# Attention and MoE on one planned instruction stream: the first batch weighted pair by pair, its pooled V summed in two halves, other staging rooms for incoming weights, and a planner that holds an engine for what is urgent

## The chip, the cores and the metric

The kernel runs on one core of a Trainium2 chip. The metric is the device time of one execution in microseconds (us), lower is better.

## What is computed

The input is q, k and v of 8 batches, 8 heads, 576 tokens and 64 channels in float32, and the weights of an MoE layer of width 512 to 2048 and back. The reference, cut to what matters:

```python
q_d, k_d, v_d = (t.reshape(B, H, 144, 4, D).mean(axis=3) for t in (q, k, v))
out_up = np.repeat(softmax(q_d @ k_d.T / 8) @ v_d, 4, axis=2)        # pooled attention
mask = np.abs(pos[:, None] - pos[None, :]) < 4
out_local = softmax(np.where(mask, q @ k.T / 8, -1e9)) @ v           # seven neighbours
x = (out_up + out_local).transpose(0, 2, 1, 3).reshape(4608, 512)
h = x @ w_in                                                         # 512 -> 2048
P = a[0] + a[1] * h + a[2] * h * h + a[3] * h**3
Q = 1.0 + abs(b[0]) * abs(h) + abs(b[1]) * h * h
out = (P / (Q + 1e-6)) @ w_out                                       # 2048 -> 512
```

The weights arrive as 64-bit floats and are turned into float32 on the chip.

## The kernel before

**A planner writes the order.** Every piece of work is a task with an engine, an estimated duration, the rooms of SBUF and PSUM that it reads and writes, and for some a due time (`add(engine, dur, fn, reads, writes, due)`). `Plan.run` walks back from the due times to a latest start for each task, and then plays the tasks through: whichever engine is free soonest takes, of its tasks whose inputs are ready by the estimates, the one with the earliest latest start. `LAG` and `OWN` are the times that the planner allows between a task and one that needs it; for SP (the DMA queue) that is the time from the end of the issue to the landing. What comes out is a fixed list for each engine, and on the chip each engine takes its list in order: an instruction that has to wait holds up all behind it.

**The MoE half** goes through ten blocks of tokens: 512 tokens of each batch, and the 64 left over of each of four batches together. A block has 16 steps (8 for the small ones). Step n makes 128 rows of h in `h_part` (TensorE, into bank 2 or 3), turns them into g = P/Q in `middle` (ScalarE reads h four times at L705, then VectorE from L720 on), and adds g times its rows of `w_out` to four output banks in `o_part` (L757). Weights and x are split in a high and a low part (`wh` and `wl`, `xs`), and a product is three matmuls. Block 0 is different: its h is a plain float32 matmul (L680) from `xf`, which holds x before the split, and `wb`, the unsplit float32 weight, so it needs neither split. Its four matmuls of a step take the four pairs of heads one after the other.

**The attention half** works on pairs of heads; a batch has four (0 to 3). For a pair: scores (L399, L409), softmax (`nm` on VectorE, exponentials `el` at L456 and `ep` at L482 on ScalarE), normalising on VectorE, turning by TensorE and copying back on ScalarE (`turned`: `ept` L543, `et` L553 and L554), then `weighted`: pooled V by the pooled attention (L579), V windows by the local one (L568), `up` (L625), and the sum of both into `xf` (L611, `put_x`). For batches 1 to 7 this is strewn into the block before. Batch 0 comes first and alone, and until its x is there TensorE has only small work; `warm` fills its gaps with matmuls that nobody reads (L889), by the gaps that the planner foresees.

**Pooled V of batch 0** (`vf`) comes by one load from SP and three adding DMAs from GpSimd (L811), each of which waits for the landing of the one before.

**The weights**: 32 chunks of 512 KB, 16 of `w_in` and 16 of `w_out`, in the order in which the steps need them. `weights` loads a chunk into a staging room (a "spot", L310), ScalarE scales it (L320), VectorE makes the float32 word in two steps (L323, L326) and, for `w_out`, ScalarE and VectorE split it (L340, L343; for `w_in` that comes later, before block 1). The staging rooms are eleven: five (`st`) lie in the rooms `m` and `g` that `middle` uses from step 0 on and serve once, four (`sl`) lie in the rooms of the last weights, two (`sx`) in the room of x of batch 1. After the first nine chunks the rest take turns in the four `sl`, and the last seven in the two `sx`.

Of the kernel before, what the change touches and what calls it, by code (L numbers as in the profile page):

```python
# [76 lines left out]
class Plan:  # L77
# [3 lines left out]
    LAG = {"PE": 0.25, "DVE": 0.14, "ACT": 0.18, "POOL": 0.2, "SP": 2.0}  # L81
# [34 lines left out]

    def run(self):
# [20 lines left out]
        while len(done) < len(self.tasks):  # L138
# [29 lines left out]
def attention_moe(  # L168
# [136 lines left out]
    def weights(w, f, spot, due=None):  # L305
# [62 lines left out]
    def load_pooled(c):

        s, b, i = c.slot, c.b, c.i  # L370
        for dst, src, cost in ((s.pq, qkp, 0.5), (c.vp, vp, 0.4)):
# [184 lines left out]
    def vp_of(c):  # L556
        return vf.ap[:, c.i] if c.b == 0 else c.vp.ap

    def weighted(cs, bk, due):
# [3 lines left out]
        def window(c, x, w, o):  # L563
            g, k = w % 2, w // 2
            nq = min(WQ, S - w * WQ)
            for j in range(2):
                m = c.pos(j) * D
                nc.tensor.matmul(  # L568
                    x.ap[j * D : (j + 1) * D, o : o + nq],
                    lhsT=c.slot.vw.ap[m : m + D, w, :],  # L570
                    rhs=c.slot.et.ap[m : m + D, k, g * D : g * D + nq],
                    start=True, stop=True, skip_group_check=True,
                )

        def part_b():
            for c, x in zip(cs, avb):
                for kc in range(2):
                    for j in range(2):
                        nc.tensor.matmul(  # L579
                            x.ap[j * D : (j + 1) * D, 256 : 256 + SD],  # L580
# [401 lines left out]
```

## Time and profile before

| | |
|---|---|
| median of 3 runs (lowest to highest) | 986.43 us (985.28 to 986.58) |
| the profiled execution | 986.62 us |
| its span, from first to last instruction | 984.9 us |
| TensorE busy (matmuls) | 961.5 us, 98% of the span |
| VectorE, ScalarE busy | 838.9 us (85%), 810.8 us (82%) |
| mean granted TensorE clock | 0.994 |

The profiled execution has 1.7 us outside its span. Times in the views are microseconds from the span's start. PE is TensorE, DVE VectorE, ACT ScalarE, POOL GpSimd, SPq the DMA queue of SP. Busy spans of neighbouring instructions overlap by some 0.1 us, so what an instruction costs in a full stretch is read from start to start.

### The profile page before, as it was taken

To read this page: it belongs to the slowest core of one execution; us is meant where nothing else is said; L and a number is where in the kernel's file an instruction comes from. 1 tells how busy PE (TensorE), PEld (TensorE's weight loads), DVE (VectorE), ACT (ScalarE), POOL (GpSimd) and SP (SyncE) were. 2 spreads that over 40 slices of the span, in tenths; PEclk is the share of its full clock that TensorE was granted. 3 is DMA by queue.
4 is the path that set the end of the run, shared out by engine and by line. 5 is a ranking of instruction groups with operands and counts; after the bars stand their busy time and mean duration, and the time that the engine had idled before them with its cause. 6 is when DMAs were issued, how large, how long until landed. Compare 5 with 4: busy or idle time off the path is not lost.

```text
span 984.9 us, 19800 instructions
## 1 busy us (share of the span) xinstructions
PE 961.5 (98%) x7379; PEld 759.3 (77%) x7379; DVE 838.9 (85%) x1472; ACT 810.8 (82%) x2078; POOL 149.2 (15%) x177
## 2 busy tenths in 40 slices
PE   7799999999999999999999999999999999999997
PEld 5556656788888888988888887888878888898886
DVE  6699999988878978887978898888888888888886
ACT  6789987897989798679797978798887979767775
POOL 1400213122222222001212030302121220000000
PEclk9989999999999999999999999999999999999999
DMA  9964544333443234003334142524233420100001
GB/s 317 297 206 142 143 135 90 89 69 71 74 118 72 68 75 105 1 22 86 64 84 120 57 81 64 107 74 67 84 60 108 74 52 1 44 1 22 1 1 43
DMA packets 46371, 83.43 MB, mean 85 GB/s; under 512 B 6564, under 2 KB 29092, under 8 KB 46276
## 3 DMA queue, kind: packets, MB, share of 16 engines
q1 hardware_dynamic: 25828, 62.70, 19.2%
q0 software_dynamic: 20448, 19.48, 14.3%
q8 instruction: 58, 0.95, 0.4%
q14 instruction: 37, 0.30, 0.1%
HBM read 72.72 MB, written 9.44 MB: 83 GB/s over the span
## 4 chain that ended last, share of the span: by engine, by line
PE 87%; DMA 5%; DVE 3%; ACT 3%; issue 0%; ACTq 0%; SPq 0%
PE psum L757 39%; PE psum L692 36%; PE psum L680 3%; DMA sl<-in_w_out_dram 3%; PE psum L568 2%; PE psum L530 2%; PE psum L579 1%; PE psum L537 1%; PE psum L409 1%; PE psum L426 1%; DMA vw<-in_vw_dram 1%; ACT m L705 1%; DMA sx<-in_w_out_dram 1%; PE psum L399 1%; DVE wl L343 1%; ACT el L456 1%
## 5 line engine op out<-in xcount | busy, mean ns | idle before, releaser
L757 PE MATMUL psum<-wh,g 128*128 128x512 f32 x1152 | 369.3, 402 | 1.2 <-DVE g L738 1.1
L692 PE MATMUL psum<-xs,wh 128*128 128x512 f32 (+1 forms) x1152 | 265.0, 370 | 0.0
L705 ACT ACTIVATE m<-psum,cf 128x512 f32<-128x512 f32 x288 | 218.7, 766 | 40.2 <-PE psum L692 37.5
L757 PEld LDWEIGHTS psum<-wh,g 128*128 128x128 f32 x1152 | 208.8, 188 | 49.2 <-issue 4.8
L692 PEld LDWEIGHTS psum<-xs,wh 128*128 128x128 f32 x1152 | 199.3, 189 | 35.9
L757 PE MATMUL psum<-wl,g 128*128 128x512 f32 x576 | 224.7, 391 | 0.0
L705 ACT ACTIVATE gb<-psum,cf 128x512 f32<-128x512 f32 x144 | 116.4, 808 | 53.4 <-PE psum L757 53.4
L376 POOL DMA_DIRECT2D pq<-in_qkp_dram x84 | 74.7, 924 | 476.0 <-DMA pq<-in_qkp_dram 449.4
L692 PE MATMUL psum<-xs,wl 128*128 128x512 f32 (+1 forms) x576 | 141.5, 367 | 0.0
L729 DVE TENSOR_TENSOR g<-m,m 128x512 fp32r<-128x512 f32 x144 | 99.2, 689 | 42.4 <-ACT m L705 40.0
L720 DVE SCALAR_TENSOR_TENSOR m<-m,cf,m 128x512 f32<-128x512 f32 x144 | 107.6, 747 | 31.5 <-ACT m L705 31.3
L757 PEld LDWEIGHTS psum<-wl,g 128*128 128x128 f32 x576 | 108.1, 188 | 23.6
L456 ACT ACTIVATE el<-psum,nm 128x64 f32<-128x64 f32 x320 | 97.8, 355 | 33.7 <-DVE nm L448 33.4
L726 DVE TENSOR_TENSOR m<-m,gb 128x512 f32<-128x512 f32 x144 | 99.3, 689 | 21.6 <-ACT gb L705 17.0
L692 PEld LDWEIGHTS psum<-xs,wl 128*128 128x128 f32 x576 | 101.3, 189 | 18.9 <-issue 1.2
L705 ACT ACTIVATE gb<-m,cf 128x512 f32<-128x512 f32 x144 | 108.0, 750 | 0.0
L732 DVE SCALAR_TENSOR_TENSOR m<-m,g 128x512 f32<-128x512 f32 x144 | 99.3, 689 | 2.9
L737 DVE TENSOR_TENSOR m<-m,m 128x512 f32<-128x512 f32 x144 | 99.3, 689 | 2.9
L725 DVE TENSOR_TENSOR m<-m,m 128x512 f32<-128x512 f32 x144 | 98.6, 685 | 0.4 <-ACT m L705 0.4
L738 DVE TENSOR_TENSOR g<-m,m 128x512 fp32r<-128x512 f32 x144 | 98.0, 680 | 0.8
L705 ACT ACTIVATE m<-gb 128x512 f32<-128x512 f32 x144 | 94.5, 656 | 2.5
L376 POOL DMA_DIRECT2D vp<-in_vp_dram x84 | 71.6, 916 | 151.7 <-DMA vp<-in_vp_dram 142.8
(66 smaller groups left out, 989.3 us busy)
## 6 DMA issues: line engine op xcount, KB each, us to landing
qk<-in_qk_dram SPq DMA_DIRECT2D x32, 590.0 KB, 5.0
pq<-in_qkp_dram POOLq DMA_DIRECT2D x84, 144.0 KB, 3.3
vw<-in_vw_dram SPq DMA_DIRECT2D x32, 320.0 KB, 3.5
out_dram<-xf SPq DMA_DIRECT2D x32, 256.0 KB, 2.3
vp<-in_vp_dram POOLq DMA_DIRECT2D x84, 72.0 KB, 3.2
sl<-in_w_in_dram SPq DMA_DIRECT2D x10, 512.0 KB, 8.1
sl<-in_w_out_dram SPq DMA_DIRECT2D x10, 512.0 KB, 10.5
pq<-in_qkp_dram SPq DMA_DIRECT2D x28, 144.0 KB, 2.2
```

The lines of the kernel that those rows point to most:

```text
L376: lambda d=dst, x=src, r=r: nc.gpsimd.dma_start(out=d.ap, in_=x[b, r, :, i], accum_op=ALU.add),
L456: nc.scalar.activation(out=s.el.ap[:, k, c.pos(j), :], in_=view[:, j, k, :], func=AF.Exp, bias=nm[:, 5 * j + k : 5 * j + k + 1], scale=sca ...
L692: nc.tensor.matmul(ph.ap[:, f * t : (f + 1) * t], lhsT=(high, low)[j][0][fc].ap[:, c, :], rhs=blk.x[i].ap[:, c, :], start=(part_ == 0 and ...
L705: add("ACT", cost, lambda: nc.scalar.activation(out=out_.ap, in_=in_, func=func, **kw), (room_in, cf, *more), (out_,))
L720: lambda: v.scalar_tensor_tensor(out=tb.ap, in0=tq.ap, scalar=b1, in1=tb.ap, op0=ALU.mult, op1=ALU.add),
L725: add("DVE", 0.61, lambda: v.tensor_tensor(out=ta.ap, in0=ta.ap, in1=tq.ap, op=ALU.mult), (ta, tq), (ta,))
L726: add("DVE", 0.61, lambda: v.tensor_tensor(out=ta.ap, in0=ta.ap, in1=u.ap, op=ALU.add), (ta, u), (ta,))
L729: add("DVE", 0.61, lambda: v.tensor_tensor(out=gh.ap, in0=ta.ap, in1=tq.ap, op=ALU.mult), (ta, tq), (gh,))
L732: lambda: v.scalar_tensor_tensor(out=tb.ap, in0=tb.ap, scalar=CONE, in1=gh.ap.bitcast(F32), op0=ALU.add, op1=ALU.mult),
L737: add("DVE", 0.61, lambda: v.tensor_tensor(out=tb.ap, in0=ta.ap, in1=tb.ap, op=ALU.subtract), (ta, tb), (tb,))
L738: add("DVE", 0.61, lambda: v.tensor_tensor(out=gl.ap, in0=tb.ap, in1=tq.ap, op=ALU.mult), (tb, tq), (gl,))
L757: nc.tensor.matmul(ob[sub].ap, lhsT=g[i].ap[:, f0 : f0 + P], rhs=flat((high, low)[j][1][fc].ap), start=(fc == 0 and m == 0), stop=(fc == N ...
```

## The change

Six things change; line numbers of the changed kernel are some 18 to 40 higher, so L320 is L338 there, L611 is L623, L340 is L358 and L705 is L743.

1. The planner's allowances for SP: 3.0 instead of 2.0 from issue to landing, and 4.5 for a load that starts before 60 (2.5 after); longer issue times for the big loads; 7.0 and 4.0 for the adding DMAs; slightly longer matmuls.
2. `HOLD`: when a task with a latest start at least 15 earlier than the one at hand becomes ready before that one would be done, the engine takes something shorter or is left free for it.
3. `weighted` of batch 0 goes pair by pair (`weighted_pooled`, then `weighted_local` at once), with the banks of `FIRST`.
4. `vf` becomes two tiles; SP loads one quarter of V into each, GpSimd adds one more into each, and `pooled_sums` adds the two halves up by twice as many matmuls (for batch 0 alone).
5. The staging rooms are five `sx` (in the room of the high part of x) and the four `sl`, all nine in turn for all chunks; the last seven chunks take the `sx`. None lies in `m` or `g` now.
6. `SPLIT_EARLY` 8 instead of 6.

```diff
-    LAG = {"PE": 0.25, "DVE": 0.14, "ACT": 0.18, "POOL": 0.2, "SP": 2.0}
+    LAG = {"PE": 0.25, "DVE": 0.14, "ACT": 0.18, "POOL": 0.2, "SP": 3.0}
...
+        if p.engine == "SP" and p.start is not None:
+            return 4.5 if p.start < 60.0 else 2.5
...
+            soon = [
+                (r, w.late) for r, _, w in waiting[e]
+                if r < at + t.dur - HOLD[0] and w.late < t.late - HOLD[1]
+            ]
+            if soon and at < HOLD[2]:
+                r = min(soon)[0]
+                fit = [o for o in open_[e] if at + o[2].dur <= r + HOLD[0]]
+                heapq.heappush(open_[e], (t.late, t.n, t))
+                if not fit:
+                    free[e] = r
+                    continue
+                o = min(fit)
...
-    vf = put("vf", [KC, NPAIR, 2, 2, D], F32, low[0][half].at)
+    vf = [put(f"vf{i}", [KC, NPAIR, 2, 2, D], F32, low[i][half].at) for i in range(2)]
...
-    spots = [put(f"st{i}", [P, 2 * DM], I32, r.at) for i, r in enumerate((mt[0], mt[2], mt[4], gt[0], gt[2]))]
+    spots = [put(f"sx{i}", [P, 2 * DM], I32, at) for i, at in enumerate((
+        xs[0][0].at, xs[0][0].at + 4096, xs[1][0].at, xs[1][0].at + 4096, xs[2][0].at))]
...
-    spots += [put(f"sx{i}", [P, 2 * DM], I32, xs[1][0].at + i * 4096) for i in range(2)]
...
-        add("SP", 1.4, load, (), (spot,), due=due)
+        add("SP", 1.65, load, (), (spot,), due=due)
...
-                    (dst,), (dst,), lag=2.8,
+                    (dst,), (dst,), lag=4.0,
...
+    def pooled_sums(c, x):
+        vs = vp_of(c)
+        for kc in range(2):
+            for n, v in enumerate(vs):
+                for j in range(2):
+                    nc.tensor.matmul(
+                        x.ap[j * D : (j + 1) * D, 256 : 256 + SD],
+                        lhsT=v[:, j, kc, :],
+                        rhs=c.slot.ept.ap[:, kc, :, c.pos(j), :],
+                        start=(kc == 0 and n == 0), stop=(kc == 1 and n == len(vs) - 1), skip_group_check=True,
+                    )
...
+    def weighted_pooled(c, y):
+
+        add("PE", 1.1, lambda: pooled_sums(c, y), (c.slot.ept, *vf), (y,))
+        keep_up(c, y)
+
+    def weighted_local(c, x, y, due):
+        add(
+            "PE", 0.7,
+            lambda: [window(c, x if w < 8 else y, w, w % 8 * WQ) for w in range(NW)],
+            (c.slot.vw, c.slot.et), (x, y),
+        )
+        put_x(c, x, 0, 0, NA, 0.55, due)
+        put_x(c, y, 0, NA, FULL, 0.12, due)
+        put_x(c, y, FULL - NA, FULL, S, 0.13, due)
...
-    spot_of = [spots[i % 9] for i in range(9)] + [spots[5 + i % 4] for i in range(len(order) - 9)]
+    spot_of = [spots[i % 9] for i in range(len(order))]
...
-        spot_of[i] = spots[9 + n % 2]
+        spot_of[i] = spots[n % 5]
...
-    add("SP", 0.8, lambda: nc.sync.dma_start(out=vf.ap, in_=vp[0, 0]), (), (vf,), due=-18)
-    for r in range(1, POOL):
+    for r, x in enumerate(vf):
+        add("SP", 0.8, lambda r=r, x=x: nc.sync.dma_start(out=x.ap, in_=vp[0, r]), (), (x,), due=-18)
         add(
             "POOL", 1.0,
-            lambda r=r: nc.gpsimd.dma_start(out=vf.ap, in_=vp[0, r], accum_op=ALU.add),
-            (vf,), (vf,), lag=4.0,
+            lambda r=r, x=x: nc.gpsimd.dma_start(out=x.ap, in_=vp[0, 2 + r], accum_op=ALU.add),
+            (x,), (x,), lag=7.0,
         )
...
-            turned(c, [bk[n] for n in ((6, 4, 5), (6, 4, 5), (2, 3, 0), (6, 1, 2))[2 * q + i]])
-        weighted(cs, [bk[n] for n in ((4, 5, 4, 5), (1, 2, 0, 3))[q]], due0 - 10.0 * (1 - q))
+            (tp, t0, t1), (x, y) = FIRST[2 * q + i]
+            turned(c, [bk[tp], bk[t0], bk[t1]])
+            weighted_pooled(c, bk[y])
+            weighted_local(c, bk[x], bk[y], due0 - 10.0 * (1 - q))
...
+HOLD = (0.1, 15.0, 2000.0)
+FIRST = (((6, 4, 5), (6, 4)), ((6, 4, 5), (6, 4)), ((2, 3, 0), (2, 3)), ((6, 1, 5), (6, 1)))
```

The first place is ScalarE in the middle of batch 0, behind the last exponentials `el3` (names with their numbers: `el3` is of pair 3, `sl0` and `sx4` are staging rooms). Before:

```order
L456 ACTIVATE el3_219,sm3_190<-psum,nm3_186 128x64 x5
L553 COPY et0_197<-psum 128x512
L320 ACTIVATE sl0_229<-sl0_229 128x512
L554 COPY et0_197<-psum 128x128
L482 ACTIVATE ep3_222,sm3_190<-psum,nm3_186 128x144 x3
L543 COPY ept1_205<-psum 72x288
L482 ACTIVATE ep2_215,sm2_189<-psum,nm2_185 128x144 x3
```

And in the changed kernel, where the scaling of a loaded chunk (L338) has moved behind the exponentials of all pairs:

```order
L474 ACTIVATE el3_219,sm3_190<-psum,nm3_186 128x64 x5
L561 COPY ept0_198<-psum 72x288
L500 ACTIVATE ep2_215,sm2_189<-psum,nm2_185 128x144 x3
L500 ACTIVATE ep3_222,sm3_190<-psum,nm3_186 128x144 x3
L571 COPY et0_197<-psum 128x512
L605 ACTIVATE up0_191<-psum 128x144
L572 COPY et0_197<-psum 128x128
L561 COPY ept2_214<-psum 72x288 x2
L338 ACTIVATE sx4_229<-sx4_229 128x512
```

The second place is VectorE where x of the last pairs is written. Before, the word of a chunk loaded into `sl1` for the second time (L323, L326) stood ahead of the six writes of pairs 2 and 3:

```order
L323 TENSOR_SCALAR wb1_3_127<-sl1_230 128x512
L326 SCALAR_TENSOR_TENSOR wb1_3_127<-sl1_230,wb1_3_127 128x512
L611 TENSOR_TENSOR xf0_1_155<-psum,up0_191 128x48
L611 TENSOR_TENSOR xf2_1_163<-psum,up0_191 128x64
L611 TENSOR_TENSOR xf0_1_155<-psum,up1_192 128x48
L611 TENSOR_TENSOR xf2_1_163<-psum,up1_192 128x64
L611 TENSOR_TENSOR xf0_1_155<-psum,up0_191 128x464
L611 TENSOR_TENSOR xf0_1_155<-psum,up1_192 128x464
```

Now pairs 2 and 1 are written before any chunk that is in its staging room's second turn, and the first such chunk (`sx1`) stands ahead of pair 3 only:

```order
L361 TENSOR_TENSOR wl1_0_120<-wb1_0_121,wh1_0_72 128x512
L623 TENSOR_TENSOR xf0_1_155<-psum,up0_191 128x464
L623 TENSOR_TENSOR xf0_1_155<-psum,up0_191 128x48
L623 TENSOR_TENSOR xf2_1_163<-psum,up0_191 128x64
L623 TENSOR_TENSOR xf0_1_155<-psum,up1_192 128x464
L623 TENSOR_TENSOR xf0_1_155<-psum,up1_192 128x48
L623 TENSOR_TENSOR xf2_1_163<-psum,up1_192 128x64
L344 SCALAR_TENSOR_TENSOR wb0_3_95<-sx3_228,wb0_3_95 128x512
```

The third place is ScalarE just ahead of the first read of h of step 0. Before, five scalings of chunks stood between `up` of the last pairs and that read; the last rows were:

```order
L320 ACTIVATE sl2_231<-sl2_231 128x512
L340 CAST wh1_4_76<-wb1_4_129 128x512
L320 ACTIVATE sl0_229<-sl0_229 128x512
L340 CAST wh0_5_61<-wb0_5_99 128x512
L320 ACTIVATE sl1_230<-sl1_230 128x512
L705 ACTIVATE m2_166<-psum,cf_181 128x512
```

Now there are two, `sx0` and `sx2`, both rooms in their second turn; `sx2` takes chunk 7 of `w_in`:

```order
L605 ACTIVATE up1_192<-psum 128x144
L571 COPY et3_220<-psum 128x512
L572 COPY et3_220<-psum 128x128
L358 CAST wh1_2_74<-wb1_2_125 128x512
L338 ACTIVATE sx0_225<-sx0_225 128x512
L358 CAST wh0_0_56<-wb0_0_89 128x512
L338 ACTIVATE sx2_227<-sx2_227 128x512
L358 CAST wh0_1_57<-wb0_1_91 128x512
L358 CAST wh1_3_75<-wb1_3_127 128x512
L358 CAST wh0_2_58<-wb0_2_93 128x512
L743 ACTIVATE m2_166<-psum,cf_181 128x512
```

## Rows read from the trace of the kernel before

**Rows 1.** Four stretches: busy PE, PEld, DVE, ACT, POOL; granted clock, DMA share, GB/s.

```profile
0.00:40.00 40.00, 30.00 (x459) 22.25 (x460) 26.95 (x60) 29.35 (x133) 7.87 (x14) 0.96 0.98 317
40.00:60.00 20.00, 14.58 (x138) 7.87 (x136) 13.82 (x30) 11.85 (x25) 6.68 (x8) 0.83 0.99 281
60.00:185.00 125.00, 122.44 (x855) 78.71 (x855) 123.31 (x228) 113.68 (x298) 21.00 (x24) 1.00 0.48 131
185.00:960.00 775.00, 775.00 (x5853) 635.50 (x5853) 658.95 (x1133) 642.49 (x1605) 113.64 (x132) 1.00 0.27 62
```

**Rows 2.** The timeline of TensorE in the first 70 us: start, length, what.

```profile
3.06 1.22 PE L889 MATMUL psum<-maskb,identb 128*128 128x256 bf16 x5 [3.06 <-DMA maskb<-in_mask_dram]
...
6.28 1.35 PE L409 MATMUL psum<-qk 64*64 64x64 f32 x40 [1.59 <-DMA qk<-in_qk_dram]
...
12.01 0.94 PE L889 MATMUL psum<-maskb,identb 128*128 128x256 bf16 x7
...
50.56 9.48 PE L680 MATMUL psum<-xf,wb 128*128 128x512 f32 x16 [4.75 <-DVE xf L611]
...
60.98 7.23 PE L680 MATMUL psum<-xf,wb 128*128 128x512 f32 x16
```

**Rows 3.** The chain of waits around 40 to 50 us: start, length, what.

```profile
40.80 7.12 DMA sl<-in_w_out_dram
...
48.00 0.68 ACT sl L320
...
49.23 0.70 DVE wb L326
```

**Rows 4.** The timeline of VectorE from 48 to 60 us.

```profile
48.70 0.50 DVE L323 TENSOR_SCALAR wb<-sl 128x512 int32<-128x512 int32 x1 [4.69 <-ACT sl L320]
...
49.84 1.67 DVE L611 TENSOR_TENSOR xf<-psum,up 128x48 f32<-128x48 f32 x6
...
54.76 0.42 DVE L323 TENSOR_SCALAR wb<-sx 128x512 int32<-128x512 int32 x1
55.10 0.69 DVE L326 SCALAR_TENSOR_TENSOR wb<-sl,wb 128x512 int32<-128x512 int32 x1
55.70 0.68 DVE L343 TENSOR_TENSOR wl<-wb,wh 128x512 fp32r<-128x512 f32 x1
...
59.62 0.75 DVE L720 SCALAR_TENSOR_TENSOR m<-m,cf,m 128x512 f32<-128x512 f32 x1
```

**Rows 5.** The timeline of ScalarE from its first exponential to its first read of h.

```profile
8.84 0.31 ACT L456 ACTIVATE el<-psum,nm 128x64 f32<-128x64 f32 x1 [6.83 <-DVE nm L448]
...
24.96 0.64 ACT L553 COPY et<-psum 128x512 f32<-128x512 f32 x1
...
42.66 0.62 ACT L340 CAST wh<-wb 128x512 fp32r<-128x512 f32 x1
43.18 0.27 ACT L554 COPY et<-psum 128x128 f32<-128x128 f32 x1
...
50.03 0.66 ACT L320 ACTIVATE sl<-sl 128x512 f32<-128x512 f32 x1 [1.03 <-DMA sl<-in_w_out_dram]
50.60 1.13 ACT L340 CAST wh<-wb 128x512 fp32r<-128x512 f32 x2
...
58.43 0.67 ACT L705 ACTIVATE m<-psum,cf 128x512 f32<-128x512 f32 x1
```

**Rows 6.** Groups of ScalarE's instructions, 8 to 58 us: busy, mean ns, idle before.

```profile
L320 ACT ACTIVATE sl<-sl 128x512 f32<-128x512 f32 x8 | 5.4, 678 | 9.1 <-DMA sl<-in_w_out_dram 6.0 <-DMA sl<-in_w_in_dram 3.0
...
L320 ACT ACTIVATE sx<-sx 128x512 f32<-128x512 f32 x3 | 2.0, 680 | 1.4 <-DMA sx<-in_w_out_dram 1.4
```

**Rows 7.** The timeline of GpSimd, its adding DMAs into pooled V.

```profile
7.92 0.99 POOL L811 DMA_DIRECT2D vf<-in_vp_dram  x1 [6.62 <-DMA vf<-in_vp_dram]
16.29 0.83 POOL L811 DMA_DIRECT2D vf<-in_vp_dram  x1 [7.38 <-DMA vf<-in_vp_dram]
```

**Rows 8.** The chain of waits between 90 and 200 us, one row.

```profile
176.93 0.66 DVE m L720
```

More of the change, by code (lines that the diff above doesn't have):

```diff
@@ L556, in vp_of, with window @@
     def vp_of(c):
-        return vf.ap[:, c.i] if c.b == 0 else c.vp.ap
+        return [x.ap[:, c.i] for x in vf] if c.b == 0 else [c.vp.ap]
+    def window(c, x, w, o):
+        g, k = w % 2, w // 2
+        nq = min(WQ, S - w * WQ)
+        for j in range(2):
+            m = c.pos(j) * D
+            nc.tensor.matmul(
+                x.ap[j * D : (j + 1) * D, o : o + nq],
+                lhsT=c.slot.vw.ap[m : m + D, w, :],
+                rhs=c.slot.et.ap[m : m + D, k, g * D : g * D + nq],
+                start=True, stop=True, skip_group_check=True,
+            )
@@ new lines, in keep_up, with put_x @@
+    def keep_up(c, x):
+        up = ups[c.p % 2]
+        add(
+            "ACT", 0.19,
+            lambda: nc.scalar.activation(out=up.ap, in_=x.ap[:, 256 : 256 + SD], func=AF.Copy, scale=1.0 / POOL),
+            (x,), (up,),
+        )
+    def put_x(c, bank, at, lo, hi, cost, due):
+        m = (hi - lo) // POOL
+        up = ups[c.p % 2]
+        if hi <= FULL:
+            xf = xsf[c.b % 2][1]
+            dst = xf.ap[:, c.i, lo:hi]
+            room = part(xf, None, 4 * (c.i * FULL + lo), 4 * (hi - lo))
+        else:
+            xf, r0 = xsf[2][1], c.b % 4 * REST
+            dst = xf.ap[:, c.i, r0 : r0 + REST]
+            room = part(xf, None, 4 * (c.i * 4 * REST + r0), 4 * REST)
+        add(
+            "DVE", cost,
+            lambda: nc.vector.tensor_tensor(
+                out=dst.rearrange("p (s r) -> p s r", r=POOL),
+                in0=bank.ap[:, at : at + hi - lo].rearrange("p (s r) -> p s r", r=POOL),
+                in1=up.ap[:, lo // POOL : hi // POOL].unsqueeze(2).broadcast_to([P, m, POOL]),
+                op=ALU.add,
+            ),
+            (bank, up), (room,), due=due,
+        )
@@ L561, in weighted @@
         ava, avb = bk[: len(cs)], bk[len(cs) :]
[L563 to L573, printed above, removed]
@@ L575, in part_b @@
         def part_b():
             for c, x in zip(cs, avb):
[L577 to L580, printed above, removed]
-                            lhsT=vp_of(c)[:, j, kc, :],
-                            rhs=c.slot.ept.ap[:, kc, :, c.pos(j), :],
-                            start=(kc == 0), stop=(kc == 1), skip_group_check=True,
-                        )
+                pooled_sums(c, x)
@@ L699, in h_part @@
             add(
-                "PE", 4 * (0.0135 + t / 2400), issue, ((high, low)[j][0][fc], blk.x[i]), (ph,),
+                "PE", 4 * (0.017 + t / 2400), issue, ((high, low)[j][0][fc], blk.x[i]), (ph,),
                 due=due_h(n) + 0.25 * f + 0.05 * part_,
@@ L766, in o_part @@
             ws = [(high, low)[j][1][fc] for j in {PROD[m][1] for m, _ in what}]
-            add("PE", 0.2285 * len(what), issue, (*gs, *ws), [ob[sub] for sub in {sub for _, sub in what}], due=due + 0.02 * q)
+            add("PE", 0.231 * len(what), issue, (*gs, *ws), [ob[sub] for sub in {sub for _, sub in what}], due=due + 0.02 * q)
     def store(k):
@@ L913 @@
 H_STEP = 6.2
-SPLIT_EARLY = 6.0
+SPLIT_EARLY = 8.0
 QUAD_GAP = 45.0
```

52 lines of the change are left out of this document (15 added, 37 removed).

## The prediction

> **What bounds the kernel now.** I read the busy times by stretch first [rows 1]. From 185 to 960 TensorE is busy 775.00 of 775.00 us: nothing can be won there without removing matmuls, and the change removes none. So time can only come from the start, and whatever the start gives shifts all that follows. From 60 to 185 TensorE is busy 122.44 of 125 and VectorE 123.31 of 125, so this stretch (block 0, with the weights and the attention of batch 1) is full on both. The first 60 us are not: TensorE has 44.6 us of small work and fillers in them, VectorE 40.8, while the DMA engines are full (shares 0.98 and 0.99, at 317 and 281 GB/s).
>
> The timeline of TensorE shows the first matmul of h at 50.56, after 4.75 us of idle that VectorE's writing of x ends [rows 2]. The chain of waits says what VectorE was late for [rows 3]: a chunk of weights issued at 40.80 took 7.12 us to land, ScalarE scaled it at 48.00, and VectorE made its word until 49.9. VectorE stood 4.69 us idle ahead of that word, and the six writes of x, whose inputs were there, came at 49.84, behind it [rows 4]. This is a queue held up by its head: the planner thought the chunk would land sooner. ScalarE is the engine that is held up most: between its first exponential at 8.84 and its first read of h at 58.43 [rows 5] lie 49.6 us, and 9.1 + 1.4 = 10.5 of them are idle time ahead of scalings that wait for chunks [rows 6].
>
> **The change part by part.**
>
> *ScalarE's list up to the first read of h.* I count it in the two orders. The attention of batch 0 is the same work. The scalings are 12 instead of 16, and the casts 7 instead of 12; the rest comes after the read. A scaling costs 0.57 (50.03 to 50.60), a cast 0.52 (42.66 to 43.18) [rows 5], so 4 x 0.57 + 5 x 0.52 = 4.9 us leave the path. Of the 49.6 us, 10.5 are waits for chunks, 39.1 the rest; 39.1 - 4.9 = 34.2 us remain.
>
> *When ScalarE begins.* The fillers before the first scores are 21 instead of 5, since the planner now believes that loads land later. Five took 1.22 us, 0.24 each; later seven took 0.94, 0.13 each, as the early ones run before the array has its full clock [rows 2]. So 21 end at 3.06 + 5.1 = 8.2 at the slow rate or 5.9 at the fast one. The four mask matmuls behind them take as long as now, so the scores, which now start at 6.28 when their load has landed, start at about 8.3 or not later than now. I take the slow end, being the nearest row, and all that ScalarE does begins 2.0 later: at 10.8. Bounds 8.8 and 10.9.
>
> *What waits are left on ScalarE.* In the first place of the order the chunk's scaling is gone from between the copies of pair 0, and the scalings that now follow the exponentials are of chunks issued among the first nine. Only rooms in their second turn can be late: `sx1`, `sx0` and, just ahead of the read of h, `sx2` with chunk 7 of w_in. The bytes ahead of that one on the queues are 12 chunks of 512 KB, five qk of 590, four windows of V of 320, V in four quarters of 288, and some 0.6 MB of small ones and adding DMAs: 12.6 to 12.9 MB. At 317 GB/s [rows 1] that is 40 to 41 us. ScalarE gets to it at 10.8 + 34.2 less one scaling and three casts, 42.9, so by bytes it has landed. But its issue also waits for a word on VectorE, and a load under this traffic took 7.12 us or more [rows 3]. I put 1.5 us of waits into the sum, for this and the small ones; bounds 0, and 10.5 if every wait only moves.
>
> The first read of h is then at 10.8 + 34.2 + 1.5 = 46.5 instead of 58.43: **11.9 us earlier**.
>
> *TensorE until then.* It does the four matmuls of h's step 0 (two instructions each) and may begin before pair 3 is done, since a step takes the pairs one after the other. `weighted` pair by pair is the same windows in the same number; pooled V in two halves doubles the pooled sums of batch 0, 16 more float32 matmuls of 144 columns, some 2 us of engine time in a stretch where TensorE has 15 us to spare [rows 1]. If that cover were gone it would cost those 2. The low clock costs something now: the first 16 matmuls of h took 9.48 against 7.23 for 16 later ones [rows 2], 2.25 us, at a granted clock of 0.83 over that stretch [rows 1]. With fillers down from 115 to 93 I count on no gain there; the read on ScalarE comes after it either way.
>
> *VectorE until then.* It does three L323, three L326 and three L343 less than now before its first L720: 3 x (0.34 + 0.60 + 0.60) = 4.6 us, from the starts at 54.76, 55.10 and 55.70 (L343 taken as L326, same shape) [rows 4]. 40.8 - 4.6 leaves 36 us to do by 46.5. It is not the bound.
>
> *Pooled V.* Now three adds run one behind the other, 8.37 us from the first to the second [rows 7], so the sum is there at about 33; then two adds run side by side after one load each. If they take no longer together than one alone, V is there at 16 to 17; if they share, at 7.92 + 2 x 8.37 = 24.7. It is first needed when `ept` of pair 0 is copied, which the order puts where the copy at 24.96 stands [rows 5], plus the 2.0: at 27. Either value is in time, so it costs and gives nothing by itself, but lets pair 0 be weighted before the others. The Trainium skill speaks against the split: "DMA: Bandwidth & Descriptors", section "Issuing engines are not separate DMA queues", says that DMAs started by different engines end on the same 16 engines and interleave, so starting two at once saves issue time only. By that rule the value is 24.7, and the sum is the same. What it leaves, a margin of 2.3 us, is where the second rival begins.
>
> *Block 0.* The stretch to follow is full on VectorE, so the shift lasts only if VectorE's work between the same landmarks does not grow. From its first L720 at 59.62 [rows 4] to that of the first step of block 1 at 176.93 [rows 8] it takes 117.3 us. In the two orders I count between these: L323 17 and now 20, L326 18 and 21, L343 23 and 16 (splits of w_in that may come later), one score maximum less (0.85), all else equal: 1.0 + 1.8 - 4.2 - 0.85 = -2.2. Four steps on it is +1.6, since the splits are due. I take 0. TensorE's own work there is unchanged, with 2.6 us of idle and the 2.25 of low clock in it; it allows a shift of some 14.
>
> *The rest.* `SPLIT_EARLY` and the planner's other numbers move work within a stretch in which TensorE never waits; the end of the list is the same. I take 0, and price it below.
>
> **Sum**: 986.62 of the profiled execution (986.43 is the median, 0.2 less) - 11.9 = **974.7 us**.
>
> **The rivals.**
>
> *The waits move along (0.25).* The DMA engines are full for the whole start, and a byte comes no sooner for a better order. If chunks for `sx1`, `sx0`, `sx2` and their issues behind VectorE come late, or if two adds side by side take longer than twice one and hold pair 0 past 27, ScalarE keeps about half its waits, 6 instead of 1.5: 979.2. For it: shares 0.98 and 0.99. Against: two chunks of the last seven, loaded early into `sx` now, no longer go ahead of urgent ones, which frees 1 MB, 3.3 us at 317 GB/s.
>
> *Better than the sum (0.07).* The clock is up early and nothing waits: 2.0 + 1.5 more, and the 2.2 of VectorE: 969.
>
> *Swallowed (0.08).* VectorE fills block 0 to 98.6% [rows 1]. If it has no work in hand when it starts earlier, because the chunks still come at the old times, its full stretch ends when it ends now: 986.
>
> *Slower (0.08).* `HOLD` puts an urgent task of TensorE ahead of one that could run, on the estimate that its input comes in time. If the input is late, TensorE stands, which it never does from 185 to 960. Batches 2 to 7 have twelve half batches of attention there. Between 60 and 185 TensorE has 2.6 us of idle [rows 1]; were each half to cost that, twelve would cost 31, and the result is 1006. It decides from 1.0 us a half. Against: now it pays none of that with shorter estimates, and the longer ones put more room before each input.
>
> **How the numbers follow.** The forecast has 0.52, with 969 to 978 from its bounds (3.5 better to 3 worse); with the better rival's upper part and most of the first rival's 978 to 983, 968 to 982 holds nearly 8 in 10. A measurement of this kernel tells 0.2%, 2 us, from no change. Faster is forecast, better, and moved waits: 0.84; same is swallowed, 0.08; slower 0.08.
>
> **What would show it.** Right: first exponential at about 10.8, first L743 near 46.5, first L758 near 48, idle before L338 under 3 us in the start, the six writes of x no longer behind a chunk, TensorE without idle after 185, and the same 117 us from the first L758 to that of block 1. The ScalarE step is wrong if idle ahead of L338 stays over 6 us. The block 0 step is wrong if the 117 grows. The last step is wrong if TensorE shows idle ahead of turns or weighted sums in later batches. What would make it all wrong is one load in the start that lands much later than its bytes say, since every list is in order.

## Result and the profile after

The changed kernel takes **976.08 us** (median of 4 runs, 975.17 to 977.32) against 986.50 for the kernel before on the same chip: a ratio of 0.9893, 95% interval 0.9881 to 0.9904, so 10.4 us faster. The profiled execution took 976.34, with a span of 974.5. The forecast was 974.7, in 968 to 982.

The windows of the changed kernel, as in [rows 1] (busy time and instructions of PE, PEld, DVE, ACT and POOL, granted clock, DMA share, GB/s):

```profile
0.00:40.00 40.00, 33.61 (x532) 25.33 (x534) 28.02 (x63) 28.72 (x134) 4.30 (x10) 1.00 0.96 330
40.00:60.00 20.00, 19.95 (x145) 10.92 (x146) 18.70 (x37) 18.46 (x41) 6.46 (x7) 1.00 1.00 294
60.00:185.00 125.00, 123.26 (x871) 82.53 (x871) 122.62 (x229) 117.35 (x303) 23.37 (x27) 0.99 0.49 127
185.00:960.00 775.00, 775.00 (x5811) 634.71 (x5810) 656.64 (x1137) 640.05 (x1593) 113.25 (x132) 1.00 0.27 61
```

TensorE's idle time up to 185 us is 8.2 us (185 less 33.61, 19.95 and 123.26), where [rows 1] have 18.0. Those 9.8 us are nearly all of the 10.4 by which the span is shorter: 9.0 lie in the first 60 us (15.4 became 6.4), 0.8 in block 0 (2.6 became 1.7). From 185 to 960 TensorE is busy all the time in both. Idle time is not the whole account, because the fillers count as busy: they went from 115 with 18.3 us to 93 with 14.0, while TensorE's other matmuls, among them twice as many pooled sums of batch 0 (5.0 us instead of 2.4), went from 943 to 947 us. That 9.8 and 10.4 agree so closely rests on these two cancelling.

TensorE's timeline (start, duration, idle time before in brackets where there is some): the fillers, the first scores, the first pooled sum, then the 16 matmuls of h's steps 0 and 1 (eight each) and the next 16, against [rows 2].

```profile
3.07 4.40 PE L929 MATMUL psum<-maskb,identb 128*128 128x256 bf16 x21 [3.07 <-DMA maskb<-in_mask_dram]
...
7.56 0.75 PE L427 MATMUL psum<-qk 64*64 64x64 f32 x40
...
24.63 0.71 PE L594 MATMUL psum<-ept,vf 72*64 72x144 f32 x8
...
38.52 1.04 PE L718 MATMUL psum<-xf,wb 128*128 128x512 f32 x2
...
41.22 1.88 PE L718 MATMUL psum<-xf,wb 128*128 128x512 f32 x4
...
44.34 4.56 PE L718 MATMUL psum<-xf,wb 128*128 128x512 f32 x10
...
49.78 7.23 PE L718 MATMUL psum<-xf,wb 128*128 128x512 f32 x16
```

The first 16 matmuls come in three pieces, between TensorE's work for the later pairs, and take 7.48 us where they took 9.48 in one piece. VectorE's timeline, against [rows 4] and [rows 8]: the last sum over four queries, two writes of x, and VectorE's first word of h at step 0 and at the first step of block 1.

```profile
19.76 1.35 DVE L405 TENSOR_REDUCE pq<-qk 128x288 f32<-128x1152 f32 x1 [0.88 <-DMA qk<-in_qk_dram]
...
38.16 0.89 DVE L623 TENSOR_TENSOR xf<-psum,up 128x464 f32<-128x464 f32 x3 [0.92 <-PE psum L582]
...
44.22 0.89 DVE L623 TENSOR_TENSOR xf<-psum,up 128x464 f32<-128x464 f32 x3 [0.81 <-PE psum L582]
...
48.42 0.75 DVE L758 SCALAR_TENSOR_TENSOR m<-m,cf,m 128x512 f32<-128x512 f32 x1 [0.23 <-ACT m L743]
...
165.19 0.74 DVE L758 SCALAR_TENSOR_TENSOR m<-m,cf,m 128x512 f32<-128x512 f32 x1
```

The writes of x now wait for TensorE's windows, no longer behind a chunk. ScalarE's groups between 8 and 48 us, as in [rows 6] (busy time and mean of one, then idle time ahead and what ended it):

```profile
L474 ACT ACTIVATE el<-psum,nm 128x64 f32<-128x64 f32 x40 | 12.1, 389 | 7.9 <-DVE nm L466 7.9
...
L338 ACT ACTIVATE sx<-sx 128x512 f32<-128x512 f32 x8 | 5.5, 710 | 0.0
...
L358 ACT CAST wh<-wb 128x512 fp32r<-128x512 f32 x7 | 4.3, 624 | 0.9 <-DVE wb L344 0.9
...
L561 ACT COPY ept<-psum 72x288 f32<-72x288 f32 x8 | 2.9, 399 | 1.9 <-PE psum L548 1.6 <-ACT et L572 0.2
L338 ACT ACTIVATE sl<-sl 128x512 f32<-128x512 f32 x4 | 2.7, 685 | 0.0
```

Ahead of scalings (the two rows of L338) the idle time is 0.0, where it was 10.5. 7.5 of the first row's 7.9 lie ahead of the first exponential. The two adds of V on POOL, against [rows 7]:

```profile
7.76 0.98 POOL L849 DMA_DIRECT2D vf<-in_vp_dram  x1 [6.45 <-DMA vf<-in_vp_dram]
9.39 0.83 POOL L849 DMA_DIRECT2D vf<-in_vp_dram  x1 [0.65 <-DMA vf<-in_vp_dram]
```

They landed at 16.20 and 18.65. The chain of waits (start, duration, what) now has the last load of Q and K early in it, and no chunk before the first read of h:

```profile
6.17 13.56 DMA qk<-in_qk_dram
...
28.12 0.74 PE psum L548 x6
...
44.40 2.79 PE psum L718 x6
47.19 0.02 issue
47.22 1.84 ACT m L743 x3
```

From 28.12 to 47.19 every piece of this chain is TensorE's. The window from 30 to 40 us shows the same:

```profile
30.00:40.00 10.00, 10.00 (x170) 7.99 (x168) 7.92 (x21) 7.52 (x20) 1.79 (x2) 1.00 0.98 331
```

So in the changed kernel TensorE, full from 30 us on, ends the wait for the first read of h. ScalarE is idle 0.34 us just ahead of that read.

### The profile page after: what moved, and what is told of

It is laid out like the page before. It is cut to its first block, busy times and chain, and to the rows that moved or that the text cites. A ratio compares the mean times of both kernels' runs of the same rounds, so it can differ in the third digit from the quotient of the medians.

```text
span 974.5 us, 19826 instructions
## 1 busy us (share of the span) xinstructions
PE 961.0 (99%) x7389; PEld 759.9 (78%) x7389; DVE 833.1 (85%) x1472; ACT 810.5 (83%) x2078; POOL 147.4 (15%) x176
## 4 chain that ended last, share of the span: by engine, by line
PE 86%; DVE 6%; ACT 4%; DMA 2%; issue 1%; ACTq 0%; SPq 0%; DVEq 0%
PE psum L795 38%; PE psum L730 37%; PE psum L582 3%; DMA qk<-in_qk_dram 2%; PE psum L594 2%; PE psum L548 2%; PE psum L555 2%; ACT m L743 2%; PE psum L427 1%; PE psum L444 1%; ACT el L474 1%; PE psum L718 1%; DVE m L770 1%; DVE g L767 1%; PE psum L417 1%
## 5 line engine op out<-in xcount | busy, mean ns | idle before, releaser
L743 ACT ACTIVATE m<-psum,cf 128x512 f32<-128x512 f32 x288 | 215.4, 753 | 44.9 <-PE psum L730 43.3
L743 ACT ACTIVATE gb<-psum,cf 128x512 f32<-128x512 f32 x144 | 115.0, 799 | 57.5 <-PE psum L795 57.5
L730 PE MATMUL psum<-xs,wl 128*128 128x512 f32 (+1 forms) x576 | 143.8, 371 | 0.0
L758 DVE SCALAR_TENSOR_TENSOR m<-m,cf,m 128x512 f32<-128x512 f32 x144 | 107.4, 746 | 0.3 <-ACT m L743 0.2
L743 ACT ACTIVATE gb<-m,cf 128x512 f32<-128x512 f32 x144 | 106.6, 740 | 1.1 <-DVE m L758 1.1
L743 ACT ACTIVATE m<-gb 128x512 f32<-128x512 f32 x144 | 93.5, 649 | 5.1 <-DVE m L763 2.7
```

The lines of the kernel that those rows point to most:

```text
L730: nc.tensor.matmul(ph.ap[:, f * t : (f + 1) * t], lhsT=(high, low)[j][0][fc].ap[:, c, :], rhs=blk.x[i].ap[:, c, :], start=(part_ == 0 and ...
L743: add("ACT", cost, lambda: nc.scalar.activation(out=out_.ap, in_=in_, func=func, **kw), (room_in, cf, *more), (out_,))
L758: lambda: v.scalar_tensor_tensor(out=tb.ap, in0=tq.ap, scalar=b1, in1=tb.ap, op0=ALU.mult, op1=ALU.add),
```

## Experiments

The theory behind the forecast, **A**: the gain comes from the planner's new numbers for loads, which take chunk work out of the way of urgent work. Rivals: **B**, the new rooms for incoming weights bring it; **C**, weighting pair by pair with V in halves; **D**, the rule that holds TensorE. When A fell, **E** to **H** were made, told with the runs that test them. Names with `m_` are the changed kernel with a part taken back, `b_` the kernel before with a part added.

All twelve in one table. "Read" is ScalarE's first read of h; "idle" TensorE's idle time from 0 to 185 us, both of the profiled execution; the ratio is to the kernel before on the same chip.

| kernel | read, us | idle, us | span, us | median, us | ratio (95% interval) |
|---|---|---|---|---|---|
| before | 58.43 | 18.0 | 984.9 | 986.5 | 1 |
| after | 47.22 | 8.2 | 974.5 | 976.08 | 0.9893 (0.9881 to 0.9904) |
| m_costs | 47.09 | 11.1 | 973.9 | 975.69 | 0.9887 (0.9872 to 0.9902) |
| m_pairs | 46.23 | 10.2 | 974.9 | 977.30 | 0.9904 (0.9889 to 0.9918) |
| m_halves | 50.33 | 9.8 | 975.7 | 977.74 | 0.9913 (0.9898 to 0.9928) |
| m_hold | 46.31 | 10.3 | 975.9 | 978.78 | 0.9924 (0.9908 to 0.9941) |
| m_spots | 47.74 | 13.9 | 982.5 | 983.32 | 0.9956 (0.9940 to 0.9972) |
| m_late2 | 48.57 | 9.8 | 977.4 | 978.98 | 0.9923 (0.9904 to 0.9941) |
| m_costs_halves | 52.87 | 17.2 | 982.6 | 984.43 | 0.9977 (0.9968 to 0.9987) |
| v_late | 47.20 | 9.2 | 976.1 | 977.64 | 0.9908 (0.9893 to 0.9923) |
| b_costs | 51.00 | 14.3 | 984.5 | 987.96 | 1.0008 (0.9999 to 1.0018) |
| b_spots | 58.46 | 19.2 | 986.8 | 989.76 | 1.0025 (1.0013 to 1.0036) |
| b_costs_spots | 51.67 | 11.8 | 980.8 | 983.55 | 0.9970 (0.9956 to 0.9984) |
| b_halves_spots | 54.39 | 16.6 | 982.8 | 984.05 | 0.9971 (0.9961 to 0.9982) |

The medians of before that belong to the ratios were 987.14 (m_costs, m_spots, b_costs, b_spots), 986.75 (m_late2 and the three kernels with two parts in their names) and 986.5 (the others); the ratios are what compares. Idle time of TensorE alone doesn't order the kernels: m_costs has 2.9 us more of it than the changed kernel and ends as early, with 72 fillers (11.8 us) instead of 93 (14.0).

**The planner's numbers, taken back and alone.**

```diff
-    LAG = {"PE": 0.25, "DVE": 0.14, "ACT": 0.18, "POOL": 0.2, "SP": 3.0}
+    LAG = {"PE": 0.25, "DVE": 0.14, "ACT": 0.18, "POOL": 0.2, "SP": 2.0}
...
-        if p.engine == "SP" and p.start is not None:
-            return 4.5 if p.start < 60.0 else 2.5
...
-        add("SP", 1.65, load, (), (spot,), due=due)
+        add("SP", 1.4, load, (), (spot,), due=due)
```

That is m_costs (with the other durations and lags, and TensorE's two costs, taken back too); b_costs makes the same edits the other way on the kernel before.

> The changed kernel with the planner's old numbers for loads (SP's lag 2.0 s and its old durations, no gap between an issue and what reads it, 2.8 for window loads, 4.0 for the adds of V) and the old costs of TensorE's groups. Everything else of the change stays. Theory A (the gain comes from the allowances for loads, which take chunk work out of the way of urgent work in the engines' lists): most of the 10.4 us is lost, 982 to 987, and ScalarE again stands idle for 6 us or more ahead of scalings of chunks that have not landed, before its first read of h. Theory B (the gain comes from the rooms of the incoming weights, through fewer bytes early): 976 to 979, with under 3 us of such idle.

> The kernel before with the new planner's numbers for loads and TensorE's groups, and nothing else of the change. Theory A: most of the gain, 976 to 980, with the first read of h at 47 to 51 and little idle ahead of scalings. Theory B: 984 to 988, since the same bytes still go early. Theory C (pair by pair and the halves of V are what lets h begin): also 984 or more, since pair 0 must still wait for pair 1 and for the third add of V, and there the idle time shows on TensorE.

m_costs loses nothing, and its first read of h is as early. Its groups of ScalarE between 8 and 48 us show next to no wait for chunks:

```profile
L336 ACT ACTIVATE sx<-sx 128x512 f32<-128x512 f32 x9 | 6.2, 704 | 0.6 <-DMA sx<-in_w_in_dram 0.6
L336 ACT ACTIVATE sl<-sl 128x512 f32<-128x512 f32 x4 | 2.7, 696 | 0.0
```

b_costs reads h 7.4 us earlier than the kernel before and yet ends within 0.2% of it. **Theory A falls**: the numbers are neither needed nor enough. Where b_costs loses its start is read from the timelines of SP, ScalarE and TensorE at the end of block 0:

```profile
130.66 0.33 SPq L312 DMA_DIRECT2D sx<-in_w_in_dram  x1
...
137.67 0.33 SPq L312 DMA_DIRECT2D sx<-in_w_out_dram  x1
...
145.39 0.33 SPq L312 DMA_DIRECT2D sx<-in_w_out_dram  x1
...
150.91 0.67 ACT L322 ACTIVATE sx<-sx 128x512 f32<-128x512 f32 x1 [0.93 <-DMA sx<-in_w_out_dram]
...
152.57 0.48 PE L532 MATMUL psum<-ident,ep 112*72 112x112 f32 x3 [2.14 <-ACT et L555]
```

The last chunks pass through two rooms, one every 7 to 8 us. ScalarE stands with the last one's scaling at the head of its list; the copies of `et` for batch 1 are behind it, and TensorE waits 2.14 us for them. VectorE's first word of the steps is 6.8 us earlier than before at step 0 and 8.2 at step 12, 2.4 at step 14.

**The rooms, taken back and alone.**

```diff
-    spots = [put(f"sx{i}", [P, 2 * DM], I32, at) for i, at in enumerate((
-        xs[0][0].at, xs[0][0].at + 4096, xs[1][0].at, xs[1][0].at + 4096, xs[2][0].at))]
+    spots = [put(f"st{i}", [P, 2 * DM], I32, r.at) for i, r in enumerate((mt[0], mt[2], mt[4], gt[0], gt[2]))]
...
+    spots += [put(f"sx{i}", [P, 2 * DM], I32, xs[1][0].at + i * 4096) for i in range(2)]
...
-    spot_of = [spots[i % 9] for i in range(len(order))]
+    spot_of = [spots[i % 9] for i in range(9)] + [spots[5 + i % 4] for i in range(len(order) - 9)]
...
-        spot_of[i] = spots[n % 5]
+        spot_of[i] = spots[9 + n % 2]
```

That is m_spots; b_spots does the reverse.

> The changed kernel with the old rooms for incoming weights and their old rotation. Theory B: 983 to 987, two more chunks go early and urgent loads land 3 us later. Theory A: 976 to 980, since the planner still allows for late loads.

> The kernel before with the new rooms for incoming weights and nothing else. Theory B: 977 to 981. Theory A: 984 to 989, the first read of h stays near 58 and idle ahead of scalings stays near 10 us.

Neither theory has both right. m_spots loses 6 us of the gain (0.9956 against 0.9893), but not by late loads in the start: its read of h is at 47.74. It loses in block 0. ScalarE's groups from 60 to 130 us in m_spots:

```profile
L338 ACT ACTIVATE sl<-sl 128x512 f32<-128x512 f32 x13 | 8.9, 700 | 3.6 <-DMA sl<-in_w_in_dram 3.6
L338 ACT ACTIVATE sx<-sx 128x512 f32<-128x512 f32 x1 | 0.7, 663 | 0.0
```

13 of 14 chunks go through the four rooms `sl` and ScalarE waits 3.6 us for them; in the changed kernel 16 go through nine rooms, with 0.2 of waits. At the end comes the queue for two rooms that b_costs shows, here in the timelines of ScalarE and TensorE of m_spots:

```profile
148.82 0.67 ACT L338 ACTIVATE sx<-sx 128x512 f32<-128x512 f32 x1 [0.56 <-DMA sx<-in_w_out_dram]
...
150.50 0.48 PE L548 MATMUL psum<-ident,ep 112*72 112x112 f32 x3 [1.73 <-ACT et L571]
```

The window of block 0 in m_spots:

```profile
60.00:185.00 125.00, 118.56 (x799) 77.91 (x798) 120.08 (x223) 111.42 (x285) 20.88 (x24) 0.97 0.51 134
```

TensorE has 6.4 us of idle time in it (1.7 after), and a clock of 0.97. b_spots alone is 0.25% slower: its read of h stays at 58.46, so there is nothing to keep.

**Pair by pair, the halves of V, and the hold, each taken back.**

```diff
...
-            weighted_pooled(c, bk[y])
-            weighted_local(c, bk[x], bk[y], due0 - 10.0 * (1 - q))
...
+        weighted(cs, [bk[n] for n in ((4, 5, 4, 5), (1, 2, 0, 3))[q]], due0 - 10.0 * (1 - q))
```

> The changed kernel with batch 0 weighted two pairs together again, in the old banks; the halves of V stay. Theory C (pair by pair lets the start run ahead): first read of h 3 us or more later than 47.2 and 979 to 984. Theory A: within 2 us of the changed kernel, 974 to 978, since h also needs pair 3 and ScalarE's list up to the read is the same work.

```diff
-    vf = [put(f"vf{i}", [KC, NPAIR, 2, 2, D], F32, low[i][half].at) for i in range(2)]
+    vf = [put("vf", [KC, NPAIR, 2, 2, D], F32, low[0][half].at)]
...
-    for r, x in enumerate(vf):
...
+    for r in range(1, POOL):
+        add(
+            "POOL", 1.0,
+            lambda r=r: nc.gpsimd.dma_start(out=vf[0].ap, in_=vp[0, r], accum_op=ALU.add),
+            (vf[0],), (vf[0],), lag=7.0,
+        )
```

> The changed kernel with pooled V added up in one tile by three adds one behind the other, which ends near 33 us instead of 18.65. Theory C: pair 0 and 1 wait for V, first read of h 5 us later, 980 to 984. Theory A: the planner moves the pooled sums behind, within 3 us, 975 to 979. If the loss is over 6 us V was on the path after all, which the prediction counted at nothing.

```diff
-HOLD = (0.1, 15.0, 2000.0)
+HOLD = (0.1, 15.0, 0.0)
```

> The changed kernel without the rule that holds TensorE for an urgent task. Theory A: 975 to 978, the same within what can be told. Theory D (the rule is what keeps fillers and h's later steps from the way of urgent turns): 980 or more. If the rule costs something, as the rival that ends slower had it, faster than the changed kernel: below 975.

m_pairs and m_halves end 1.1 and 2.0 us behind the changed kernel by their ratios, and the intervals overlap: with the new numbers there, C falls. In m_pairs V is there at 17.91, but its first pooled sum begins at 32.32, and yet its first read of h is the earliest of all: an early V is not in itself what makes the read early. m_hold is slower by 0.3% (2 to 3 us), which is less than D asked for and the opposite of the rival that the hold costs time. One place where it shows, on TensorE's timeline of m_hold:

```profile
172.10 1.20 PE L730 MATMUL psum<-xs,wh 128*128 128x512 f32 x4 [1.65 <-ACT gb L743]
```

**The second half of V later.**

```diff
-        add("SP", 0.8, lambda r=r, x=x: nc.sync.dma_start(out=x.ap, in_=vp[0, r]), (), (x,), due=-18)
+        add("SP", 0.8, lambda r=r, x=x: nc.sync.dma_start(out=x.ap, in_=vp[0, r]), (), (x,), due=(-18, -11.5)[r])
```

> The changed kernel with the load of the second half of V issued behind the last load of Q and K of batch 0 instead of ahead of the first, so that 288 KB less stands ahead of that load, which landed at 19.7 us (16.9 in the kernel before). If that landing is on the path, as the chain of waits has it, the last load of Q and K lands 0.9 us or more earlier, the first read of h comes 1 to 3 us earlier, 973 to 975. If it is not, 976, the same. If the second add then comes too late for the pooled sums of pair 0 (over 27 us), 977 to 980.

The last sum over four queries begins at 18.40 with no wait for its load (19.76 after), the first read of h at 47.20 (47.22). The load early in the chain of the changed kernel is not what sets the read: in v_late the chain runs along ScalarE, its exponentials above all, up to 26.5 and then along TensorE, and the two reads are 0.02 us apart. The second add landed at 27.05 and the pooled sums began at 27.33 instead of 24.63. 977.64 lies in the range expected for a V that is late, but the first read of h is not later; the 1.6 us by which the profile ends later come in block 0, where TensorE has 3.1 us of idle time instead of 1.7. The two intervals overlap, so all that can be told is that nothing is gained.

**Second round.** So far: only the rooms are missed much when taken back alone, and neither of the two parts tried alone brings anything. **E**: the early start is kept only if the last chunks do not queue for two rooms, the waits that b_costs and m_spots share. **H**: in the start, V is late unless it comes in halves, and the planner knows it is late only by the new numbers; one of the two must be there. **F** and **G** are their rivals.

```diff
-        spot_of[i] = spots[n % 5]
+        spot_of[i] = spots[2 + n % 2]
```

> The changed kernel, but its last four or so chunks of weights of each matrix pass through two rooms (those that the kernel before had) instead of five; the start is the same to the instruction. Theory E (the early start is kept only if the last chunks of w_out, at 115 to 150 us, do not queue for two rooms): the first step's words on VectorE at 48.4 as in the changed kernel, and 3 us or more lost between 130 and 175 us, 979 to 984, with idle time of TensorE behind a scaling of the last chunk. Rival F (what the old rooms cost in the earlier run was the early chunks in the rooms of the middle's own tiles): 975 to 977.

m_late2 is 0.3% slower than the changed kernel, at the edge of what E expected, and its last chunks come as in b_costs (SP's issues and ScalarE):

```profile
133.40 3.13 SPq L328 DMA_DIRECT2D sx<-in_w_out_dram  x2
...
143.25 0.33 SPq L328 DMA_DIRECT2D sx<-in_w_out_dram  x1
...
148.20 0.68 ACT L338 ACTIVATE sx<-sx 128x512 f32<-128x512 f32 x1 [0.23 <-DMA sx<-in_w_out_dram]
```

The changed kernel issues its last chunk at 127.42 and scales it at 152.86 with no wait. In the profiles m_late2 ends 2.8 us later; 1.35 of them were there at step 0 already, from the clock (last section), and 1.5 come behind it, where m_spots loses 7.5. But behind step 0 it is the changed kernel that has a stretch of low clock, as its window and then that of m_late2 show:

```profile
150.00:160.00 10.00, 8.32 (x117) 6.29 (x116) 8.99 (x18) 7.93 (x17) 3.34 (x4) 0.83 0.37 77
150.00:160.00 10.00, 7.40 (x154) 5.43 (x153) 9.24 (x19) 9.73 (x20) 3.46 (x5) 1.00 0.48 78
```

So the clock took something from both, and the 1.5 is too small a price for the two rooms. By the medians m_late2 loses 2.9 us and m_spots 7.2, by the ratios 0.30% and 0.63%: E stands for two fifths to a half of what the old rooms cost. The rest belongs to what m_late2 leaves new: nine rooms in turn instead of four, for which the 3.6 us of waits in m_spots speak, and the early chunks outside the middle's tiles (F). These two were not taken apart.

m_costs_halves makes the edits of m_costs and m_halves together, and the two `b_` kernels those edits on the kernel before that their names say.

> The changed kernel with the old planner's numbers and with pooled V in one tile by three adds. Its ScalarE has 11 scalings and 3 casts ahead of the first read of h (12 and 7 in the changed kernel, 16 and 12 in the kernel before). Theory G (the work on chunks ahead of the read sets the start): read at 46 to 49, 975 to 978. Rival H (with V late the list before the read stands still until the third add has landed at 33 or later; either the new numbers or the halves of V had to be there): read at 51 or later, 979 to 984.

> The kernel before with both the new planner's numbers and the new rooms, neither of which gained anything alone; no pair by pair, no halves of V, no rule that holds TensorE. Theory E: the numbers bring the start 6 to 8 us forward and the rooms keep it, 978 to 981. If the two do not belong together: 985 or more.

> The kernel before with pooled V in two halves and the new rooms, nothing else. Its ScalarE has 16 scalings and 12 casts ahead of the first read of h, as many as the kernel before. Theory G: read at 56 or later, and no gain, 984 to 990. Rival H: V is there at 17 to 19 us instead of 33, read at 49 to 53, and the rooms keep it, 977 to 981.

m_costs_halves decides for **H**. Without the numbers 975.69, without the halves 977.74, without both 984.43. TensorE and ScalarE of m_costs_halves:

```profile
32.10 1.23 PE L592 MATMUL psum<-ept,vf 72*64 72x144 f32 x8 [7.72 <-DMA vf<-in_vp_dram]
...
33.37 0.29 ACT L603 ACTIVATE up<-psum 128x144 f32<-128x144 f32 x1 [8.03 <-PE psum L592]
```

Behind that wait the granted clock is low too, 0.55 from 30 to 40 us; the window from 0 to 40:

```profile
0.00:40.00 40.00, 25.78 (x359) 19.73 (x360) 19.67 (x43) 21.38 (x115) 5.91 (x13) 0.83 0.93 317
```

It has the shortest list of all, 11 scalings and 3 casts ahead of the read, and a late read, since everything stands for V. m_halves has 15 and 12 and reads at 50.33: there the planner knows of the late V and puts chunk work into the wait. That work is not lost, VectorE and ScalarE must do it in block 0 otherwise; so a read 3.1 us later costs 1.7 in the median. H holds for a kernel that weights pair by pair: the kernel before has neither the numbers nor the halves, its V landed at 32.01, and its first pooled sum, at 32.85, did not wait for it. Which part of the wait pair by pair brings was not tested. And the new rooms don't by themselves keep a start: of the 5.5 us by which m_costs_halves is ahead of the kernel before at step 0, 2.3 are left at the end.

b_costs_spots, of two parts that gain nothing alone, gains 3.2 us (0.9970), but not the 6 to 8 expected. Its start is 6.7 earlier at step 0 and 6.3 at step 24, so the rooms keep what the numbers bring, as E has it, and b_costs, without them, keeps 2.0 of its 6.8 to step 24. Then 2.2 are lost between 217 and 924 us. TensorE's timeline shows half of it, 0.18 to 0.19 us once in each of six of the later blocks:

```profile
831.43 0.50 PE L759 MATMUL psum<-wh,g 128*128 128x512 f32 x1 [0.19 <-DVE g L740]
```

The window of the later blocks in b_costs_spots has 1.1 us of idle time, where it was 0 in the kernel before:

```profile
185.00:960.00 775.00, 773.88 (x5840) 632.10 (x5839) 652.64 (x1128) 639.79 (x1591) 113.24 (x132) 1.00 0.28 62
```

b_costs has the same six, no kernel with `m_` has. So the new numbers cost something in the later blocks that another part of the change takes away. m_hold and m_pairs don't have them either, so it is neither of these two alone; `SPLIT_EARLY` was not tried.

b_halves_spots fits neither expectation: read at 54.39, between the two, and a gain of 2.9 us. V is there at 19.12, but TensorE's list has the first pooled sum at 33.73, so the early V is not used. ScalarE still has as many scalings and casts as in the kernel before, and waits for chunks:

```profile
L320 ACT ACTIVATE sx<-sx 128x512 f32<-128x512 f32 x10 | 7.3, 727 | 1.0 <-DMA sx<-in_w_out_dram 0.9
L320 ACT ACTIVATE sl<-sl 128x512 f32<-128x512 f32 x6 | 4.2, 700 | 2.6 <-DMA sl<-in_w_in_dram 2.1 <-DMA sl<-in_w_out_dram 0.5
```

No version was found that beats the changed kernel by more than can be told: m_costs equals it with fewer edits.

## Why the prediction was right, step by step

**Only the start counts.** Right: TensorE is busy for all 775 us of the rest, and the shift at 205 to 225 us (9.8) is that at the end (10.3).

**ScalarE begins 2.0 later.** 0.7 later: 9.54, not 10.8. The 21 fillers took 4.40, 0.21 each, between the two rates that bounded it. The reason given for the slow rate, the array's clock, doesn't show in the trace: the granted clock is 1.00 from 0 to 40 us.

**ScalarE's list is 4.9 shorter.** From first exponential to read there are 37.67 us, 4.31 of them idle, so 33.4 of work, against 49.58 with 11.24 idle and 38.3 of work: 5.0 less. The size was right. As a cause it was wrong: m_costs_halves has a shorter list and reads 5.7 us later, m_halves a list nearly as long as before and reads 8.1 us earlier than before. The list is what the planner puts into the waits.

**1.5 us of waits left.** Ahead of scalings 0.0, but other waits, which I had left in "the rest" at 0.8, grew to 4.3, of them 1.9 for the turns of `ept`. The stretch was 2.0 longer than I had it, and with the earlier beginning the **first read of h** came at 47.22, 0.7 late: 11.2 gained instead of 11.9.

**TensorE until then.** This step failed, and that it didn't move the sum is luck. I had the path on ScalarE and TensorE with 15 us to spare, so that the doubled pooled sums were covered. In the changed kernel TensorE is the path from 28 us on and full from 30 on, and the pooled sums of three pairs lie on the chain. How much earlier the read would be without their doubling was not tried.

**Pooled V gives nothing by itself.** This step failed too, though it didn't move the sum. The row has 18.65, close to the bound without sharing. The other value, 24.7, was worked out by the rule of the Trainium skill that DMAs interleave on the same 16 engines whichever engine started them ("DMA: Bandwidth & Descriptors", section "Issuing engines are not separate DMA queues"); the trace doesn't show that value. It would not have had the margin of 2.3 us either, since the first pooled sum stands at 24.63 and not at 27. Bytes ahead of a load do count elsewhere: the last load of Q and K, behind 288 KB more, is used at 19.76 in the changed kernel, at 17.75 and 18.21 in the two with one tile. What I left out is the other side: with three adds V is there at 32, and this price is 7.72 us unless the planner fills it.

**Block 0 taken as 0.** 116.8 us from the first L758 to that of block 1, against 117.3. Right in size, but without what it hangs on: the rooms, which I priced at nothing there. With the old ones and an early start the stretch is 122.7 in m_spots and 119.0 in b_costs, and the time comes back to 983 and 988. It is 119.2 in b_spots and b_halves_spots and 119.3 in m_costs_halves too, all with the new rooms, so the rooms are not the only thing that sets it. In m_spots and b_costs it is the rival called *swallowed*, chunks that keep an earlier start from lasting; the changed kernel escapes it by the part that I took for a matter of 1 MB.

**The planner's allowances.** The argument rested on them throughout; m_costs shows that they are not needed, b_costs that they are not enough.

**The hold.** The rival of 1006 was wrong in sign: without the hold the kernel is 2 to 3 us slower.

**Two sums** don't come out as written: the bytes that were listed add up to 12.4 MB and not 12.6 to 12.9, and 3.5 better than 974.7 is 971 and not 969. Neither moves the forecast.

Against its own execution the sum missed by 1.6 us (976.34): 0.7 in the read of h, and 0.9 behind it, since of 11.2 us at step 0 there are 10.3 at the end. One thing is seen there: behind 1.06 and 0.62 us of idle TensorE the granted clock is 0.50 from 154 to 156 us. So the number was right, and the gain is in the start as forecast; but the waits that were left came out 2.0 larger and the beginning 1.3 earlier than I had them; that the two nearly cancel is luck.

## What to carry to other kernels

Parts of a change to a planned order are not terms of a sum: here two ways of dealing with a late V replace each other, and with the old rooms most of an early start was lost again before the end. To price one part, take it out of the changed kernel and put it alone into the kernel before; where the two differ, look at the pair. A long list ahead of a landmark is no cost where the list is what the planner put into a wait; ask which wait it fills. And when the waits of one engine go, look which engine the chain runs along then: here it moved from ScalarE and its chunks to TensorE.

## What the runs showed of the hardware

Up to 80 us m_late2 has the same instructions in the same order as the changed kernel on every engine, and reads h 1.35 us later. The windows of m_late2, then those of the changed kernel, from 26 us on:

```profile
26.00:28.00 2.00, 1.24 (x14) 0.71 (x10) 1.14 (x5) 2.00 (x12) 0.00 (x0) 1.00 1.01 393
28.00:30.00 2.00, 1.97 (x10) 1.75 (x10) 1.93 (x5) 1.23 (x5) 0.00 (x0) 0.51 1.01 401
30.00:32.00 2.00, 2.00 (x41) 1.83 (x40) 0.36 (x1) 2.00 (x5) 0.00 (x0) 0.64 1.03 409
```

```profile
26.00:28.00 2.00, 1.33 (x14) 0.80 (x11) 1.14 (x5) 2.00 (x13) 0.00 (x0) 1.00 1.02 384
28.00:30.00 2.00, 1.88 (x32) 1.60 (x34) 1.93 (x5) 1.79 (x6) 0.00 (x0) 1.00 1.03 410
```

Behind nearly the same stretch, with TensorE busy for 1.24 and 1.33 of 2 us, the granted clock fell to the level of 1.2 GHz in one and stayed at 2.4 in the other. A difference of 1.4 us in the start of one profile is therefore no verdict on an edit. The second thing: two adding DMAs of 288 KB begun 1.6 us apart took 8.44 and 9.25 us, little more than one alone, 8.37 from one to the next [rows 7], in a stretch in which the DMA engines were busy 0.96 of the time.
